# Memory attention and a SiLU feed-forward layer on one core: the gate table by one copy, the first head's loads on another queue, the last sums block by block

## The chip, the core and the metric

The kernel runs on one core of a Trainium2 chip. The core has TensorE (PE in the profile, its weight loads PEld), VectorE (DVE), ScalarE (ACT), GpSimd (POOL) and SyncE (SP). SyncE only issues loads and stores here. SBUF holds the tiles, PSUM the results of TensorE. The metric is the time of one execution in microseconds (us); lower is better.

## The reference

For 8 batches and 8 heads, q, k and v have 576 rows of 64 columns. All is float32.

```python
scores = scale * np.matmul(q, k.transpose(0, 1, 3, 2))        # causal mask, softmax -> a
local = np.matmul(a, v)
q_p = phi(q)                                                   # elu(q) + 1
mem_out = einsum(q_p, M_prev) / (einsum(q_p, z_prev) + 1e-6)
g = 1.0 / (1.0 + np.exp(-beta))                                # one gate for each head
x = g * mem_out + (1 - g) * local                              # -> [4608, 512]
h = x @ w_in                                                   # 512 -> 2048
return (h * (1.0 / (1.0 + np.exp(-h)))) @ w_out                # 2048 -> 512
```

## The kernel before, in words

**Tiles.** A head is worked in `scores` (its softmax and its phi) and `values` (its sums over v and M_prev). Its q and k come in as `raw`, 32 columns at a time, by four loads (L193); DVE transposes the tile (L221, `tt`), and ScalarE copies the q half beside it (L224, `qf`), after which TensorE can start the head's scores (L250). Each block of 128 score rows is reduced on DVE with the mask (L252) and turned into probabilities on ScalarE (L254, the last 64 rows L294). POOL divides them by the sums (L304). `raw` has one buffer, so the four loads of a head wait until the head before has been transposed. There are two PSUM buffers for scores. The first ten heads are worked in plain float32 (`whole`); the others split each operand into a high and a low part.

**The other loads of a head.** `load_rest` issues eight loads for a head: q by rows (`qn`, L201 and L202), v (`vr`, L204 and two at L206), M_prev twice (`mr`, L209) and z_prev (`zb`, L211). All go through SyncE's queue, as the weights do (L138) and all stores. `load_rest` also leaves the last of them in `anchor["sp"]`, behind which the next weight load is placed.

**The gate table.** `bet` holds beta; ScalarE and DVE make 1 + exp(-beta) and 1 + exp(beta) of it (L92 to L95). `over` (L96) repeats these for five blocks of rows and each head: POOL does it in 16 instructions, which add the value to a stretch of `mask` that is zero (L99). `over` is read at L299 and L331.

**Weights.** Each of the 32 weight slices is loaded as 64-bit words, made into float32 by ScalarE (L150, L158), DVE (L152, L154, L159) and POOL (L156), and split in two (L161, L162). Twelve slices go to a scratch in DRAM and flow in again for every block of tokens (`flow`, L485), with two buffers.

**Feed-forward.** 256 tokens are a block; there are 18. For each pair of slices of w_in, TensorE makes h (L552), ScalarE, DVE and POOL make g of it (L563 to L568), and `second` adds g times two slices of w_out to two sums `acc` of 128 tokens each (L532): for each slice c, for each block t of 128 tokens, three products. At the end ScalarE copies both sums (L578) and SyncE stores them (L580).

**What sets the order.** The program is written as generators that take turns: steps of attention, weights at a given rate, and feed-forward at a given rate. A scheduler then orders the instructions of each engine, so any edit can move instructions everywhere. An engine works its instructions in that order. Loads share eight semaphores in turn (DMAHW0 to DMAHW7 in the rows of the order): a load that takes one which an earlier load still holds waits until that load has landed.

## Time and profile before

| | us |
|---|---|
| three runs | 1330.49, 1333.85, 1334.98 (median 1333.85) |
| profiled execution | 1331.87 |
| its span in the profile | 1330.1 |
| TensorE busy | 1269.9 (95%) |
| VectorE busy | 963.4 (72%) |
| ScalarE busy | 805.2 (61%) |
| GpSimd busy | 798.1 (60%) |
| granted TensorE clock, mean | 0.978 |

Times in a profile count from the start of the span. A row of the timeline gives the start, the time taken, the engine with the line, the operation and the tiles (written <- read), how many instructions are merged, and in brackets how long the engine sat idle before it and what it waited for. SPq is SyncE's queue: the row says how long it was issuing, and landing comes later.

### The profile page before, as it was taken

To read this page: it belongs to the slowest core of one execution; us is meant where nothing else is said; L and a number is where in the kernel's file an instruction comes from. 1 tells how busy PE (TensorE), PEld (TensorE's weight loads), DVE (VectorE), ACT (ScalarE), POOL (GpSimd) and SP (SyncE) were. 2 spreads that over 40 slices of the span, in tenths; PEclk is the share of its full clock that TensorE was granted. 3 is DMA by queue.
4 is the path that set the end of the run, shared out by engine and by line. 5 is a ranking of instruction groups with operands and counts; after the bars stand their busy time and mean duration, and the time that the engine had idled before them with its cause. 6 is when DMAs were issued, how large, how long until landed. Compare 5 with 4: busy or idle time off the path is not lost.

```text
span 1330.1 us, 24649 instructions
## 1 busy us (share of the span) xinstructions
PE 1269.9 (95%) x7858; PEld 1084.7 (82%) x7858; DVE 963.4 (72%) x2580; ACT 805.2 (61%) x1999; POOL 798.1 (60%) x1169
## 2 busy tenths in 40 slices
PE   6988989999999999999999999999999999999998
PEld 2343458898989899899989898989898889899997
DVE  7988985788888878877888787778878875322222
ACT  6777765667676767667776676666767663111111
POOL 6888994676666667766677665656576653101110
PEclk9986799999999999999999999999999999999999
DMA  6766555554555545555555455455545432444444
GB/s 163 191 177 176 151 152 159 136 140 134 135 150 137 151 116 135 152 137 151 136 149 140 136 139 136 131 149 136 137 134 145 128 101 80 155 137 155 156 159 143
DMA packets 302994, 190.39 MB, mean 143 GB/s; under 512 B 258832, under 2 KB 267024, under 8 KB 302864
## 3 DMA queue, kind: packets, MB, share of 16 engines
q1 hardware_dynamic: 302864, 188.82, 50.8%
q8 instruction: 62, 1.02, 0.3%
q14 instruction: 68, 0.56, 0.1%
HBM read 173.02 MB, written 15.73 MB: 142 GB/s over the span
## 4 chain that ended last, share of the span: by engine, by line
PE 71%; DVE 13%; ACT 6%; DMA 4%; issue 3%; POOL 2%; SPq 1%; DVEq 0%; POOLq 0%; ACTq 0%
PE h L552 27%; PE acc L532 24%; PE x L422 7%; PE s L250 5%; PE tp L376 4%; DVE s L252 2%; PE x L414 1%; PE tq L351 1%; DMA zb<-in_z_prev 1%; DVE xu L505 1%; DMA flow<-wo_s 1%; DVE th L564 1%; DVE wy L152 1%; DVE wy L159 1%; ACT p L254 1%
## 5 line engine op out<-in xcount | busy, mean ns | idle before, releaser
L552 PE MATMUL h<-xu,wi 128*128 128x256 f32 x2592 | 373.8, 287 | 10.0 <-DVE th L564 7.3
L552 PEld LDWEIGHTS h<-xu,wi 128*128 128x128 f32 x2592 | 342.6, 191 | 24.9 <-DVE th L564 5.9
L304 POOL TENSOR_SCALAR p<-p,st 128x384 f32<-128x384 f32 (+3 forms) x320 | 186.1, 600 | 127.4 <-DVE st L302 121.2
L532 PE MATMUL acc<-wo,g 128*128 128x512 f32 x864 | 244.8, 399 | 0.0
L567 POOL TENSOR_SCALAR g<-th 128x512 fp32r<-128x512 f32 x144 | 90.9, 631 | 236.8 <-DVE th L564 205.7
L532 PE MATMUL acc<-flow,g 128*128 128x512 f32 x864 | 230.9, 395 | 0.7 <-DMA flow<-wo_s 0.7
L254 ACT ACTIVATE p<-s,st 128x128 f32<-128x128 f32 (+3 forms) x256 | 134.9, 528 | 123.2 <-DVE st L252 93.7
L564 DVE SCALAR_TENSOR_TENSOR th<-th,h 128x512 f32<-128x512 f32 x144 | 98.5, 685 | 130.5 <-ACT th L563 128.0
L532 PEld LDWEIGHTS acc<-flow,g 128*128 128x128 f32 x864 | 158.9, 188 | 33.9 <-DMA flow<-wo_s 1.8
L532 PEld LDWEIGHTS acc<-wo,g 128*128 128x128 f32 x864 | 150.0, 189 | 20.1 <-POOL p L304 0.5
L563 ACT ACTIVATE th<-h 128x512 f32<-128x512 f32 x144 | 85.6, 595 | 128.1 <-PE h L552 127.3
L407 DVE TENSOR_TENSOR pl<-tp,ph 128x384 fp32r<-128x384 f32 x216 | 118.4, 550 | 38.1 <-ACT ph L406 33.9
L568 DVE TENSOR_TENSOR g<-th,g 128x512 fp32r<-128x512 f32 x144 | 104.8, 728 | 50.5 <-POOL g L567 49.3
L252 DVE CUSTOM_DVE_ANT_0 s<-s,mask 128x128 f32<-128x128 f32 (+3 forms) x256 | 125.4, 492 | 11.5 <-PE s L250 6.7
L376 PE MATMUL tp<-ident,p 128*128 128x128 f32 x640 | 123.0, 292 | 8.5 <-DVE qp L359 3.7
L552 PE MATMUL h<-xu,flow 128*128 128x256 f32 x864 | 126.7, 284 | 0.0
L406 ACT CAST ph<-tp 128x384 fp32r<-128x384 f32 x216 | 104.7, 490 | 23.6 <-PE x L422 14.7
L552 PEld LDWEIGHTS h<-xu,flow 128*128 128x128 f32 x864 | 114.1, 190 | 0.9 <-issue 0.3
L376 PEld LDWEIGHTS tp<-ident,p 128*128 128x128 f32 x640 | 81.5, 147 | 37.4 <-POOL p L304 9.3
L235 POOL TENSOR_TENSOR ql<-tt,qq 64x512 fp32r<-64x512 f32 x54 | 73.2, 1356 | 20.6 <-ACT qq L231 11.3
L328 POOL TENSOR_TENSOR r<-e,zb 128x320 f32<-128x320 f32 x64 | 59.8, 935 | 42.4 <-DVE e L327 35.4
L422 PE MATMUL x<-pl,vs 128*128 128x256 f32 x324 | 81.7, 307 | 0.0
(103 smaller groups left out, 2430.2 us busy)
## 6 DMA issues: line engine op xcount, KB each, us to landing
flow<-wo_s SPq DMA_DIRECT2D x144, 512.0 KB, 3.5
flow<-wi_s SPq DMA_DIRECT2D x72, 512.0 KB, 3.8
raw<-in_k SPq DMA_DIRECT2D x128, 72.0 KB, 2.3
raw<-in_q SPq DMA_DIRECT2D x128, 72.0 KB, 2.5
out<-o SPq DMA_DIRECT2D x36, 256.0 KB, 4.2
wraw<-in_moe_w_in SPq DMA_DIRECT2D x16, 512.0 KB, 4.4
qn<-in_q SPq DMA_DIRECT2D x64, 128.0 KB, 2.9
vr<-in_v SPq DMA_DIRECT2D x64, 128.0 KB, 2.6
```

The source lines that it names most:

```text
L252: anchor["dve"] = nc.vector.tensor_tensor_reduce(s, s, mask[:, 3 * P - P * i:], QS, 3.0e38, ALU.add, ALU.min, st[:, i:i + 1]).ins
L254: nc.scalar.activation(pt, s, AF.Exp, bias=st[:, i:i + 1], scale=-1.0, accum_out=st[:, 10 + i:11 + i])
L304: nc.gpsimd.tensor_scalar(pb[x], pb[x], st[:, 15 + x:16 + x], 1.0, op0=ALU.mult, op1=ALU.mult)
L376: nc.tensor.transpose(t[:, o:o + P], pb[i][:, P * j:P * j + P], ident)
L406: nc.scalar.copy(ph[:, 0:o], t[:, 0:o])
L407: nc.vector.tensor_tensor(out=pl[:, 0:cut], in0=t[:, 0:cut], in1=f(ph[:, 0:cut]), op=ALU.subtract)
L422: nc.tensor.matmul(x[0:rows, q0:n], vs[0:n_k, j], part[0:n_k, o:o + n - q0], start=False, stop=last)
L532: nc.tensor.matmul(acc[t], ta, tb, start=p == 0 and c == 0 and n == 0, stop=p == NP - 1 and c == 1 and n == len(terms) - 1)
L552: nc.tensor.matmul(h[:, c], ta, tb, start=kk == 0 and n == 0, stop=kk == KD - 1 and n == len(terms) - 1)
L564: nc.vector.scalar_tensor_tensor(out=th, in0=th, scalar=1.0, in1=h, op0=ALU.add, op1=ALU.mult)
L567: nc.gpsimd.tensor_scalar(hi, th, 1.0, 1.0, op0=ALU.mult, op1=ALU.mult)
L568: nc.vector.tensor_tensor(out=lo, in0=th, in1=f(hi), op=ALU.subtract)
```

## The change

Three places change. `over` is now made by one POOL copy from `bet`, broadcast over the five blocks. `load_rest` issues the eight loads of the very first head on ScalarE's queue, and in that case does not set `anchor["sp"]`. In the last pair of slices of the last block of tokens, `second` fetches both slices first and then does all six products of one block of 128 tokens before those of the other; and of the last block's two sums the second is copied by VectorE.

```diff
     over = const.tile([P, 2, H, NQ], F32, name="over")
-    for j in range(2):
-        for hh in range(H):
-            nc.gpsimd.tensor_scalar(over[:, j, hh], mask[:, 0:NQ], bet[:, j, hh:hh + 1], None, op0=ALU.add)
+    nc.gpsimd.tensor_copy(
+        over.rearrange("p j h c -> p (j h) c"),
+        bet.rearrange("p j (h o) -> p (j h) o", o=1).to_broadcast([P, 2 * H, NQ]))
...
     def load_rest(b, h):
+        queue = nc.scalar if b == h == 0 else nc.sync
         qn = qrest[(b * H + h) % 2]
-        nc.sync.dma_start(out=qn[:, 0:NQ - 1], in_=q[b, h, 0:(NQ - 1) * P].rearrange("(c p) d -> p c d", p=P))
+        queue.dma_start(out=qn[:, 0:NQ - 1], in_=q[b, h, 0:(NQ - 1) * P].rearrange("(c p) d -> p c d", p=P))
...
-        anchor["sp"] = nc.sync.dma_start(out=zb, in_=z_prev[b, h:h + 1].to_broadcast([P, D])).ins
+        last = queue.dma_start(out=zb, in_=z_prev[b, h:h + 1].to_broadcast([P, D])).ins
+        if queue is nc.sync:
+            anchor["sp"] = last
...
             def second(p, g):
+                def product(c, t, w):
+                    at = slice(t * P, (t + 1) * P)
+                    terms = [(g[:, gi, c, at], w[:, wi]) for gi, wi in ((0, 0), (0, 1), (1, 0))]
+                    for n, (ta, tb) in enumerate(terms):
+                        nc.tensor.matmul(
+                            acc[t], ta, tb, start=p == 0 and c == 0 and n == 0,
+                            stop=p == NP - 1 and c == 1 and n == len(terms) - 1)
+
+                if u == NU - 1 and p == NP - 1:
+
+                    both = [fetch("o", 2 * p + c) for c in range(2)]
+                    for t in range(T // P):
+                        for c in range(2):
+                            product(c, t, both[c])
+                    return
...
-                nc.scalar.activation(o, acc[t], AF.Copy, scale=0.5)
+                if u == NU - 1 and t % 2:
+                    nc.vector.tensor_scalar(o, acc[t], 0.5, None, op0=ALU.mult)
+                else:
+                    nc.scalar.activation(o, acc[t], AF.Copy, scale=0.5)
```

The scheduler turns this into the following orders. First ScalarE at the program's start, before; the names are the tiles of the sections above, and in brackets stand the semaphores that an instruction waits for.

```order
L93 ACT_TABLE_LOAD [waits DMAHW0_49]
L93 ACTIVATE bet<-bet 128x8 [waits DVE_49]
L94 ACTIVATE bet<-bet 128x8
L224 COPY qf<-tt 64x576 [waits DVE_49]
L150 ACTIVATE wraw<-wraw 128x512 [waits DMAHW5_49]
L325 ACTIVATE e<-qn_146 128x320 [waits DMAHW7_49,DMAHW6_49,Pool_49]
```

And the same place now (line numbers of the changed file are 3 higher from L196 on):

```order
L202 DMA qn_131<-in_q 128x4x64
L203 DMA qn_131<-in_q 64x64
L93 ACT_TABLE_LOAD [waits DMAHW1_49]
L93 ACTIVATE bet<-bet 128x8 [waits DVE_49]
L94 ACTIVATE bet<-bet 128x8
L205 DMA vr<-in_v 128x4x64
L207 DMA vr<-in_v 64x64 x2
L210 DMA mr<-in_M_prev 64x64 [waits DMAHW3_49]
L210 DMA mr<-in_M_prev 64x64 [waits DMAHW5_49]
L212 DMA zb<-in_z_prev 128x64 [waits DMAHW7_49]
L227 COPY qf<-tt 64x576 [waits DVE_49]
L150 ACTIVATE wraw<-wraw 128x512 [waits DMAHW2_49]
```

The eight loads stand ahead of the first head's copy, six of them behind the exponentials of beta, and three of those wait for a semaphore of an earlier load. On SyncE the same eight are gone from between the first and the second weight slice; this is SyncE's start now:

```order
L91 DMA bet<-in_beta 128x8
L193 DMA raw<-in_k 32x18x32 x2
L193 DMA raw<-in_q 32x18x32
L193 DMA raw<-in_q 32x18x32 [waits DMAHW0_49]
L138 DMA wraw<-in_moe_w_in 128x4x128 [waits DMAHW2_49]
L138 DMA wraw<-in_moe_w_in 128x4x128 [waits DMAHW4_49]
L193 DMA raw<-in_k 32x18x32 [waits DMAHW6_49,DMAHW0_49,DVE_49]
L193 DMA raw<-in_k 32x18x32
L193 DMA raw<-in_q 32x18x32 [waits DMAHW1_49]
L193 DMA raw<-in_q 32x18x32 [waits DMAHW2_49]
```

The fourth load of the first head's `raw` now waits for the load that held DMAHW0, which is ScalarE's first; the second head's `raw` waits as before for DVE's transposition, and its last load for the first weight slice.

The second place is ScalarE further on, before: p_218 to p_249 are the first head's probabilities, blocks one to four, and the copy at L224 is the second head's.

```order
L254 ACTIVATE p_218,st<-s,st 128x128
L254 ACTIVATE p_223,st<-s,st 128x256
L161 CAST wi_114<-wy 128x512
L254 ACTIVATE p_233,st<-s,st 128x384
L150 ACTIVATE wraw<-wraw 128x512
L158 ACTIVATE wraw<-wraw 128x512
L254 ACTIVATE p_249,st<-s,st 128x512
L325 ACTIVATE e<-qn_147 128x320
L326 ACTIVATE r<-qn_147 128x320
L356 COPY qp<-tq 64x3x128
L356 COPY qp<-tq 64x2x128
L224 COPY qf<-tt 64x576
```

Now, with p_203 to p_234 for the same four blocks:

```order
L257 ACTIVATE p_203,st<-s,st 128x128
L257 ACTIVATE p_208,st<-s,st 128x256
L161 CAST wi_99<-wy 128x512
L328 ACTIVATE e<-qn_132 128x320
L227 COPY qf<-tt 64x576
L329 ACTIVATE r<-qn_132 128x320
L257 ACTIVATE p_218,st<-s,st 128x384
L158 ACTIVATE wraw<-wraw 128x512
L257 ACTIVATE p_234,st<-s,st 128x512
```

The second head's copy of q has moved from behind the first head's fourth block to ahead of its third.

The third place is TensorE at the program's end, before: wo_142 and wo_144 are slices of w_out that stay in SBUF, flow one that was loaded again.

```order
L532 MATMUL acc<-flow,g 128x512 x6
L532 MATMUL acc<-wo_142,g 128x512 x4
L552 MATMUL h<-xu,flow 128x256 x12
L532 MATMUL acc<-wo_142,g 128x512 x2
L532 MATMUL acc<-flow,g 128x512 x6
L532 MATMUL acc<-wo_144,g 128x512 x6
L532 MATMUL acc<-flow,g 128x512 x6
```

Now:

```order
L533 MATMUL acc<-flow,g 128x512 x6
L565 MATMUL h<-xu,flow 128x256 x12
L533 MATMUL acc<-wo_127,g 128x512 x6
L533 MATMUL acc<-flow,g 128x512 x6
L533 MATMUL acc<-wo_129,g 128x512 x5
L533 MATMUL acc<-flow,g 128x512 x3
L533 MATMUL acc<-wo_129,g 128x512
L533 MATMUL acc<-flow,g 128x512 x3
```

The first block's sum now has its last product four from the end, where it was three from the end.

More of the change, by code (lines that the diff above doesn't have):

```diff
@@ L199, in load_rest @@
     def load_rest(b, h):
+        queue = nc.scalar if b == h == 0 else nc.sync
         qn = qrest[(b * H + h) % 2]
-        nc.sync.dma_start(out=qn[:, 0:NQ - 1], in_=q[b, h, 0:(NQ - 1) * P].rearrange("(c p) d -> p c d", p=P))
-        nc.sync.dma_start(out=qn[0:LAST, NQ - 1], in_=q[b, h, S - LAST:S])
+        queue.dma_start(out=qn[:, 0:NQ - 1], in_=q[b, h, 0:(NQ - 1) * P].rearrange("(c p) d -> p c d", p=P))
+        queue.dma_start(out=qn[0:LAST, NQ - 1], in_=q[b, h, S - LAST:S])
         vr = pool.tile([P, NQ, D], F32, tag="vr", name="vr", bufs=3)
-        nc.sync.dma_start(out=vr[:, 0:NQ - 1], in_=v[b, h, 0:(NQ - 1) * P].rearrange("(c p) d -> p c d", p=P))
+        queue.dma_start(out=vr[:, 0:NQ - 1], in_=v[b, h, 0:(NQ - 1) * P].rearrange("(c p) d -> p c d", p=P))
         for p0 in (0, LAST):
-            nc.sync.dma_start(out=vr[p0:p0 + LAST, NQ - 1], in_=v[b, h, (NQ - 1) * P:S])
+            queue.dma_start(out=vr[p0:p0 + LAST, NQ - 1], in_=v[b, h, (NQ - 1) * P:S])
         mr = pool.tile([P, D], F32, tag="mr", name="mr", bufs=NB["mr"])
         for p0 in (0, 64):
-            nc.sync.dma_start(out=mr[p0:p0 + 64], in_=M_prev[b, h])
+            queue.dma_start(out=mr[p0:p0 + 64], in_=M_prev[b, h])
         zb = pool.tile([P, D], F32, tag="zb", name="zb", bufs=NB["zb"])
-        anchor["sp"] = nc.sync.dma_start(out=zb, in_=z_prev[b, h:h + 1].to_broadcast([P, D])).ins
+        last = queue.dma_start(out=zb, in_=z_prev[b, h:h + 1].to_broadcast([P, D])).ins
+        if queue is nc.sync:
+            anchor["sp"] = last
         return qn, vr, mr, zb
@@ L528, in second @@
                     for t in range(T // P):
-                        at = slice(t * P, (t + 1) * P)
-                        terms = [(g[:, gi, c, at], w[:, wi]) for gi, wi in ((0, 0), (0, 1), (1, 0))]
-                        for n, (ta, tb) in enumerate(terms):
-                            nc.tensor.matmul(
-                                acc[t], ta, tb, start=p == 0 and c == 0 and n == 0,
-                                stop=p == NP - 1 and c == 1 and n == len(terms) - 1)
+                        product(c, t, w)
                     if ("o", 2 * p + c) in FLOW:
```

## The prediction

> **What bounds the kernel now.** I read the page first (busy shares), then the table of windows, then the chain of waits over the first 60 us, then the timeline of the first 24 us and of the last 10 us. The page gives the whole:
>
> ```profile
> PE 1269.9 (95%) x7858; PEld 1084.7 (82%) x7858; DVE 963.4 (72%) x2580; ACT 805.2 (61%) x1999; POOL 798.1 (60%) x1169
> ```
>
> The 95% is an average over stages with different limits. The next rows give, for each stretch, its length, the busy time of each engine with its count of instructions, the granted TensorE clock, the DMA share and GB/s:
>
> ```profile
> 0.00:20.00 20.00, 9.58 (x18) 3.67 (x19) 11.68 (x40) 10.77 (x25) 13.26 (x32) 1.00 0.55 121
> 20.00:60.00 40.00, 36.44 (x81) 14.93 (x81) 36.10 (x85) 28.52 (x68) 32.55 (x29) 1.00 0.73 198
> 80.00:200.00 120.00, 102.58 (x377) 54.29 (x377) 106.53 (x232) 90.39 (x218) 109.72 (x105) 0.79 0.61 168
> 200.00:1100.00 900.00, 876.33 (x5876) 798.71 (x5875) 722.90 (x2059) 616.05 (x1561) 593.60 (x933) 1.00 0.51 138
> 1100.00:1330.00 230.00, 225.35 (x1448) 204.52 (x1447) 70.99 (x129) 43.36 (x92) 33.56 (x57) 1.00 0.43 142
> ```
>
> In the first 20 us no engine is full: PE works 9.58 us, DVE 11.68 us. From 20 to 60 us DVE (36.10 of 40) and PE (36.44) are nearly full; from 80 to 200 us DVE (106.53 of 120) and POOL (109.72) are. From 200 us on PE sets the pace: 876.33 of 900, then 225.35 of 230. So the kernel is a row of full stretches after a start that is not full and before an end of about 4 us without PE. The change touches only the start and the end. What it is worth is how much earlier or later the full stretch begins, and how much sooner the last row is stored.
>
> The chain of waits at the start (start, duration, what):
>
> ```profile
> 10.78 2.38 SPq L193
> ...
> 17.53 0.58 SPq L211
> 18.16 5.21 DMA wraw<-in_moe_w_in
> 23.39 0.43 DVE wy L152
> ...
> 24.39 2.13 POOL p L304 x3
> ```
>
> SP's queue carries the chain: it issues load after load until 18.16 us, then the third w_in slice takes 5.21 us to land, and the normalisation of the first head's probabilities (L304) starts at 24.39 us behind the DVE work on that slice. The timeline of the start has the prices:
>
> ```profile
> 1.45 0.15 POOL L112 MEMSET qn<- 64x64 f32 x1
> 3.79 0.51 SPq L201 DMA_DIRECT2D qn<-in_q  x1
> 4.75 0.19 ACT L94 ACTIVATE bet<-bet 128x8 f32<-128x8 f32 x1
> 4.94 0.58 SPq L204 DMA_DIRECT2D vr<-in_v  x1
> 5.25 5.38 POOL L99 TENSOR_SCALAR over<-mask,bet 128x5 f32<-128x5 f32 x16 [2.35 <-DVE bet L95]
> 5.85 0.78 DVE L221 STREAM_TRANSPOSE tt<-raw 128x576 f32<-128x576 f32 x1 [0.44 <-DMA raw<-in_q]
> 6.66 0.67 ACT L224 COPY qf<-tt 64x576 f32<-64x576 f32 x1 [1.72 <-DVE tt L221]
> 7.38 1.65 PE L250 MATMUL s<-tt,qf 64*128 64x128 f32 x4 [7.38 <-ACT qf L224]
> 8.04 0.58 SPq L211 DMA_DIRECT2D zb<-in_z_prev  x1
> 8.12 0.69 DVE L154 SCALAR_TENSOR_TENSOR wy<-wraw,wy 128x512 uint32<-128x512 uint32 x1
> 9.22 0.97 SPq L193 DMA_DIRECT2D raw<-in_k  x2
> 10.60 1.28 POOL L156 TENSOR_TENSOR wy<-wy,wraw 128x512 uint32<-128x512 uint32 x1
> 13.17 0.58 ACT L254 ACTIVATE p<-s,st 128x384 f32<-128x384 f32 x1
> 15.21 1.07 POOL L334 TENSOR_TENSOR e<-e,nrm 128x320 f32<-128x320 f32 x1 [0.60 <-DVE nrm L333]
> 16.56 0.77 DVE L221 STREAM_TRANSPOSE tt<-raw 128x576 f32<-128x576 f32 x1
> 18.53 0.49 DVE L284 CUSTOM_DVE_ANT_0 pair<-s,mask 64x320 f32<-64x320 f32 x1 [1.20 <-PE s L271]
> 18.66 0.67 ACT L224 COPY qf<-tt 64x576 f32<-64x576 f32 x1
> 23.39 0.43 DVE L152 TENSOR_SCALAR wy<-wraw 128x512 uint32<-128x512 uint32 x1 [0.80 <-DMA wraw<-in_moe_w_in]
> ```
>
> **Gate table.** Sixteen POOL instructions take 5.38 us (L99). One copy of 80 columns replaces them. The trace has no such copy: a 64x64 fill takes 0.15 us and the 128x320 product with a broadcast operand (L334) 1.07 us; I take 0.3 us, a quarter of L334, which has four times the columns. So POOL is freed of about 5.1 us (4.3 to 5.2). What stood behind it is L156, the first weight slice's sum, which began at 10.60 us while its DVE operand was ready at 8.81 us (8.12 + 0.69): at most 1.8 us gained. But L156 also needs ScalarE's L150, and that now stands behind the loads costed next and ends after 10 us. I cost this part at nothing: what covers it is ScalarE. If that cover is gone, it is 1.8 us on one weight slice, of which DVE waits.
>
> **First head's loads on ScalarE's queue.** The order shows two loads ahead of the exp table's load and six between L94 and the first copy of q. ScalarE is done with L94 at 4.94 us (4.75 + 0.19). The same six loads take SP from 4.94 to 8.62 us in the trace (L204 to L211, 8.04 + 0.58), 3.68 us. At SP's price ScalarE reaches its copy at 8.6 us, not 6.66 us. Two of the six also wait for a semaphore that an earlier load holds: the second M_prev load for the first v load. These are landings, from issue, of two v loads of that size (KB each, us to landing), and of the last q quarter of the second head:
>
> ```profile
> vr<-in_v SPq DMA_DIRECT2D x1, 128.0 KB, 3.7
> ...
> vr<-in_v SPq DMA_DIRECT2D x1, 128.0 KB, 2.3
> ...
> raw<-in_q SPq DMA_DIRECT2D x2, 72.0 KB, 4.4
> ```
>
> So v lands at 7.2 to 8.6 us, and the second M_prev load, which would go at 7.4 us, waits up to 1.3 us. The copy starts at 8.6 to 9.9 us: the first score of the kernel comes 2.0 to 3.3 us later, and I take 2.6. If ScalarE issues at almost no cost (no row shows it issuing), the raw loads decide: their last quarter now waits for the first q load's landing (0.72 + 2.3 = 3.0 us) where it was issued at 2.71, so +0.3. The bounds are +0.3 and +3.3. All of the first head is queued behind that copy: PE had nothing before it, and DVE's first reduction waits for PE.
>
> SP in turn is free of eight loads, from 3.79 to 8.62 us, 4.8 us. Not all comes through. The second head's raw tile has one buffer, so its load still waits for the first head's transposition; that ends at 6.63 us (5.85 + 0.78) now and 0.3 to 1 us later after, so the load goes about 2 us earlier than 9.22. Its last quarter then waits for the first w_in slice to land. At 4.4 us to landing the second head's raw is there about 2 us sooner than the trace's 15.2 us (10.78 + 4.4). Behind it SP's eight loads for the second head follow without a gap, and the third w_in slice goes about 4 us before 18.16 us.
>
> The order puts the second head's copy of q ahead of the first head's third exp on ScalarE. That exp now waits for the second head's data: 13.2 us plus 0.78 transposition plus 0.67 copy plus ScalarE's Relu beside it is about 15.5 to 16 us, where the trace has 13.17. So the first head is 2.5 to 3 us late, and the second head's copy, at 15 us for 18.66, is 3 to 4 us early. The two share DVE, which is full from 20 us on. What counts is therefore DVE's idle time until then: +2.6 us before the first reduction; minus the 1.20 us that it waited for PE at 18.53; minus the 0.80 us that it waited for the third w_in slice at 23.39. That is +0.6 us. The bounds: the lane waits at their worst and neither idle saved, +3.3; the whole 4 us by which SP is ahead carried through, -4.
>
> The Trainium skill, "Trainium Kernel Development and Optimization", section "Key Constraints", says that loads issued from SP and ACT run on the same 16 DMA engines, and that issuing from several engines saves only the issue time. The trace agrees so far as it can: a 72 KB load took 4.4 us to land after an issue of half a microsecond. By the rule the gain on SP could be no more than the issue time of the eight loads; it is the reason to doubt the 2 us on the second head's landing, and the second rival prices that.
>
> **End.** The last rows of the timeline and of the chain, an earlier DVE row, and the landing of the last store:
>
> ```profile
> 1301.08 0.69 DVE L564 SCALAR_TENSOR_TENSOR th<-th,h 128x512 f32<-128x512 f32 x1 [6.98 <-ACT th L563]
> ...
> 1325.26 1.29 ACT L578 ACTIVATE o<-acc 128x512 f32<-128x512 f32 x2 [3.99 <-PE acc L532]
> 1325.88 1.03 SPq L580 DMA_DIRECT2D out<-o  x2
> ```
>
> ```profile
> 1321.49 4.44 PE acc L532 x18
> ...
> 1325.95 0.60 ACT o L578
> ```
>
> ```profile
> out<-o SPq DMA_DIRECT2D x1, 256.0 KB, 2.6
> ```
>
> PE does its last 18 products in 4.44 us, 0.247 us each. The second copy starts at 1325.95, right behind PE's last product (1321.49 + 4.44 = 1325.93): ScalarE, done with the first copy by then, did not hold it up. A second engine for it removes a wait that is not there. DVE reading a 128x512 PSUM tile takes 0.69 us (L564), ScalarE 0.60, so that copy is up to 0.1 us longer. By the order, four products instead of three follow the first block's last one, so the first store goes 0.25 us earlier and is less in the way of the second, whose 2.6 us end the run. I take -0.2 us, bounds -0.5 and +0.3. The last weight tile is needed one product sooner; if it is not there, that is 0.25 us more.
>
> **The rest of the program.** The order is shifted everywhere by the scheduler, but heads, weight slices and FFN products keep their places to within a few dozen products. In 200 to 1100 us PE idles 23.7 us of 900; another order of the same work can move this by a few microseconds either way. I take 0, bounds -4 and +4.
>
> **Sum.** +0 (table) + 0.6 (start) - 0.2 (end) + 0 = +0.4 us. The profiled execution took 1331.87 us, its span 1330.1; so 1332.3 by its own time. The median shown, 1333.85, lies 2 us above it; on that, 1334.2 us.
>
> **Rivals.**
> One, SP's lead carries through (faster): third slice and third head arrive 4 us sooner, and so does all that follows the 18.16 us row in the chain. For it: the chain from 10.78 to 23.39 us is SP and a load it issued. Against: DVE's own work in the first 24 us waits on the first head's scores, which come later. Time 1333.85 - 4.0 - 0.2 = 1329.7, on the edge of what can be told; with a favourable order below it.
>
> Two, ScalarE's queue holds the first head up (slower): if the second head's raw lands as late as now, 15.2 us, because the DMA engines and not the issue limit it, its transposition ends at 17.33 us (16.56 + 0.77), its copy at 18.0, and the first head's third exp goes at 18.5 instead of 13.17: +5.3, less the 0.80 saved on the third slice, +4.5 us. Time 1338.4. It decides once that landing is later than about 14.7 us; every microsecond beyond adds one.
>
> Three, the granted clock (slower). This is the wait ahead of the first stretch of the profile with a granted clock below 1:
>
> ```profile
> 86.15 0.79 PE L250 MATMUL s<-tt,qf 64*128 64x128 f32 x2 [3.70 <-DVE st L284]
> ```
>
> PE idled 3.70 us, and from 80 to 200 us the mean granted clock is 0.79, 25 us of full clock lost, most of it beside full DVE and POOL. If the new order puts such an idle at 190 us or later, where PE sets the pace, 10 us at half clock cost 5 us: 1339. For it, every order of those heads is a new draw; against, from 200 us on the clock is 1.00 with PE 97% busy. The Trainium skill, "TensorE: Matmul & The Clock Gate", Part 1, says that an idle window of about 3.4 us halves the clock; the 3.70 us row agrees.
>
> **Chances.** About 0.3%, 4 us, is what a measurement of this kernel can tell from no change. The forecast 0.48, rival one 0.28, two 0.15, three 0.09. Rival one lies at the bound and the forecast's order term reaches over it on both sides; so faster 0.31, within 0.46, slower 0.23. The range takes in rival one with 2.5 us of the order term and two and three: 1327.0 to 1339.5.
>
> **What would show it.** Right: first score near 10 us, second head's copy near 15 us ahead of the first head's third exp, DVE's busy time by 26 us within 1 us of before, the last copy right behind PE's last product, PE idle of 200 to 1100 us near 24 us. Wrong: a first score before 8.5 us (ScalarE issues cheaply), a third w_in slice that no one waits for with L304 of the first head before 22 us (rival one), the second head's raw after 14.7 us (rival two), a granted clock below 1 after 200 us (rival three).

## The result, and the profile after

The changed kernel is slower. Five executions took 1349.08 to 1358.90 us (median 1350.79), the kernel before beside them 1333.61 us (median of six); the ratio of the mean times is 1.0146, 95% interval 1.0116 to 1.0175. The forecast was 1334.2 us, and the range ended at 1339.5. A sixth execution of the changed kernel, at a mean granted clock of 0.469, took 2688.68 us and is in no comparison. The profiled execution took 1358.90 us, the slowest of the five and 8.1 us above their median, so its profile shows more loss than the usual execution has; its span is 1357.1 us, 27.0 longer than before.

The busy shares of the page after:

```profile
PE 1291.7 (95%) x7858; PEld 1094.6 (81%) x7858; DVE 968.3 (71%) x2581; ACT 804.8 (59%) x1998; POOL 794.0 (59%) x1154
```

TensorE runs the same 7858 products, but is busy 21.8 us longer (1291.7 against 1269.9) and idle only 5.3 us longer (65.5 against 60.2). So most of the loss is products that took longer. The same stretches as in the prediction show where (length, busy time of PE, PEld, DVE, ACT, POOL, granted clock, DMA share, GB/s):

```profile
0.00:20.00 20.00, 7.96 (x15) 3.05 (x15) 13.18 (x37) 10.51 (x24) 8.54 (x18) 1.00 0.65 152
20.00:60.00 40.00, 32.55 (x86) 13.65 (x85) 36.13 (x87) 29.23 (x70) 30.82 (x29) 1.00 0.68 181
...
80.00:200.00 120.00, 111.23 (x328) 50.13 (x326) 100.03 (x213) 83.22 (x201) 95.27 (x90) 0.64 0.57 158
200.00:1100.00 900.00, 871.00 (x5775) 790.75 (x5775) 709.55 (x2013) 608.85 (x1538) 598.01 (x930) 0.99 0.51 136
```

From 80 to 200 us the clock fell from 0.79 to 0.64, and 328 products were done where it had been 377. From 200 to 1100 us TensorE did 101 products fewer (5775 for 5876), with 5.3 us more idle time and a clock below 1.

The chain of waits at the start, after (start, duration, what):

```profile
0.73 3.42 DMA qn<-in_q
4.17 0.31 SPq L193
...
4.53 4.54 DMA wraw<-in_moe_w_in
...
13.44 0.77 DVE tt L224
```

SyncE's queue is off it from 9 us on. What heads it is the first load on ScalarE's queue: the fourth `raw` load waits for that one to land (0.73 + 3.42 = 4.15), as the order said it would. The timeline has the rest:

```profile
3.62 0.37 ACTq L205 DMA_DIRECT2D vr<-in_v  x1
...
5.32 0.25 POOL L97 COPY over<-bet 128x80 f32<-128x80 f32 x1 [2.41 <-DVE bet L95]
6.54 0.59 ACTq L212 DMA_DIRECT2D zb<-in_z_prev  x1
...
6.66 0.78 DVE L224 STREAM_TRANSPOSE tt<-raw 128x576 f32<-128x576 f32 x1 [1.40 <-DMA raw<-in_q]
...
7.47 0.67 ACT L227 COPY qf<-tt 64x576 f32<-64x576 f32 x1 [2.42 <-DVE tt L224]
...
8.19 1.64 PE L253 MATMUL s<-tt,qf 64*128 64x128 f32 x4 [8.19 <-ACT qf L227]
...
10.38 1.29 POOL L156 TENSOR_TENSOR wy<-wy,wraw 128x512 uint32<-128x512 uint32 x1 [4.81 <-DVE wy L154]
...
13.44 0.77 DVE L224 STREAM_TRANSPOSE tt<-raw 128x576 f32<-128x576 f32 x1
...
14.56 0.67 ACT L227 COPY qf<-tt 64x576 f32<-64x576 f32 x1
...
15.74 0.43 SPq L138 DMA_DIRECT2D wraw<-in_moe_w_in  x1
...
16.30 0.58 ACT L257 ACTIVATE p<-s,st 128x384 f32<-128x384 f32 x1 [0.58 <-DVE st L255]
...
21.20 0.67 ACT L150 ACTIVATE wraw<-wraw 128x512 uint32<-128x512 uint32 x1 [1.07 <-DMA wraw<-in_moe_w_in]
...
28.19 1.36 POOL L156 TENSOR_TENSOR wy<-wy,wraw 128x512 uint32<-128x512 uint32 x1 [1.56 <-DVE wy L154]
...
30.84 1.69 POOL L156 TENSOR_TENSOR wy<-wy,wraw 128x512 uint32<-128x512 uint32 x1 [1.28 <-ACT wi L161]
...
33.93 3.81 POOL L307 TENSOR_SCALAR p<-p,st 128x128 f32<-128x128 f32 x5
```

The second head's transposition is 3.1 us earlier (13.44 for 16.56), its copy 4.1 us. But the first head's probabilities are divided by their sums at 33.93 us. Before, the same five instructions stand here:

```profile
24.01 3.07 POOL L304 TENSOR_SCALAR p<-p,st 128x128 f32<-128x128 f32 x5 [1.45 <-DVE st L302]
```

That is 9.9 us later, where the head's third exponential is only 3.1 us later (16.30 for 13.17). GpSimd did not wait for these probabilities (the last row of after has no bracket); other work stood ahead of them, and waited itself (L156, 1.56 and 1.28 us). The order of GpSimd, before, behind the first slice's L162:

```
L334 TENSOR_TENSOR e<-e,nrm 128x320
L156 TENSOR_TENSOR wy<-wy,wraw 128x512
L162 TENSOR_TENSOR wi_115<-wy,wi_115 128x512
L328 TENSOR_TENSOR r<-e,zb 128x320
L304 TENSOR_SCALAR p_218<-p_218,st 128x128
```

and after:

```
L337 TENSOR_TENSOR e<-e,nrm 128x320
L156 TENSOR_TENSOR wy<-wy,wraw 128x512
L331 TENSOR_TENSOR r<-e,zb 128x320
L162 TENSOR_TENSOR wi_100<-wy,wi_100 128x512
L337 TENSOR_TENSOR e<-e,nrm 128x320
L156 TENSOR_TENSOR wy<-wy,wraw 128x512 x3
L162 TENSOR_TENSOR wi_101<-wy,wi_101 128x512
L307 TENSOR_SCALAR p_203<-p_203,st 128x128
```

Work on weights and on the second head, whose data now come early, was put ahead of the first head. The end is as forecast:

```profile
1352.52 0.60 ACT L594 ACTIVATE o<-acc 128x512 f32<-128x512 f32 x1 [4.64 <-PE acc L533]
1352.55 0.85 PE L533 MATMUL acc<-flow,g 128*128 128x512 f32 x3
...
1353.44 0.69 DVE L592 TENSOR_SCALAR o<-acc 128x512 f32<-128x512 f32 x1 [3.34 <-PE acc L533]
```

**By heads.** A head begins where DVE transposes its `raw`; I cut both spans at the starts of heads 4, 10, 17, 32, 48 and 63 (counted from 0), so that the pieces hold about the same work. Three of the seven pieces of the table of windows, before:

```profile
0.00:56.77 56.77, 43.00 (x91) 17.35 (x92) 44.62 (x114) 36.13 (x84) 43.23 (x60) 1.00 0.69 180
56.77:156.98 100.21, 86.79 (x269) 40.77 (x269) 86.75 (x207) 78.46 (x190) 85.92 (x77) 0.79 0.63 174
...
511.40:780.81 269.41, 265.42 (x1795) 242.90 (x1794) 220.14 (x634) 189.68 (x480) 186.40 (x290) 1.00 0.53 141
```

and after:

```profile
0.00:52.77 52.77, 34.20 (x74) 13.59 (x75) 42.30 (x107) 33.62 (x78) 35.36 (x43) 1.00 0.68 177
52.77:170.06 117.29, 105.48 (x287) 45.91 (x287) 100.88 (x214) 82.87 (x199) 86.75 (x78) 0.64 0.56 153
...
525.01:803.73 278.72, 268.30 (x1786) 244.63 (x1785) 222.32 (x629) 187.61 (x474) 181.98 (x288) 0.99 0.51 135
```

Head 4 begins 4.0 us sooner, but TensorE has done 74 products by then, not 91. Heads 4 to 10 take 17.1 us longer and hold the missing ones. Heads 32 to 48, a thousand products later and far from anything that was edited, take 9.3 us longer. The pieces differ by -4.0, +17.1, -1.9, +2.4, +9.3, -0.5 and +4.6: +11.2 up to head 17, +15.8 behind it.

### The profile page after: what moved, and what is told of

Same layout as the page of the kernel before. It is cut to its first block, busy times and chain, and to the rows that moved or that the text cites. A ratio compares the mean times of both kernels' runs of the same rounds, so it can differ in the third digit from the quotient of the medians.

```text
span 1357.1 us, 24701 instructions
## 1 busy us (share of the span) xinstructions
PE 1291.7 (95%) x7858; PEld 1094.6 (81%) x7858; DVE 968.3 (71%) x2581; ACT 804.8 (59%) x1998; POOL 794.0 (59%) x1154
## 4 chain that ended last, share of the span: by engine, by line
PE 63%; DVE 16%; POOL 7%; ACT 6%; issue 5%; DMA 2%; SPq 0%; DVEq 0%; POOLq 0%; ACTq 0%
PE h L565 23%; PE acc L533 20%; PE x L425 6%; PE s L253 5%; PE tp L379 4%; POOL p L307 2%; DVE s L255 2%; PE x L417 1%; DVE th L577 1%; DVE pl L410 1%; DVE tt L224 1%; DVE xu L508 1%; PE tq L354 1%; ACT p L257 1%; DVE wy L159 1%
## 5 line engine op out<-in xcount | busy, mean ns | idle before, releaser
L565 PEld LDWEIGHTS h<-xu,wi 128*128 128x128 f32 x2592 | 346.9, 193 | 27.4 <-DVE th L577 7.7
L533 PE MATMUL acc<-wo,g 128*128 128x512 f32 x864 | 240.7, 398 | 0.0
L533 PE MATMUL acc<-flow,g 128*128 128x512 f32 x864 | 234.1, 397 | 0.7 <-DMA flow<-wo_s 0.7
L307 POOL TENSOR_SCALAR p<-p,st 128x384 f32<-128x384 f32 (+3 forms) x320 | 190.1, 613 | 74.3 <-DVE st L305 58.8
L257 ACT ACTIVATE p<-s,st 128x128 f32<-128x128 f32 (+3 forms) x256 | 135.0, 528 | 132.3 <-DVE st L255 118.8
L577 DVE SCALAR_TENSOR_TENSOR th<-th,h 128x512 f32<-128x512 f32 x144 | 98.5, 684 | 118.7 <-ACT th L576 116.7
L576 ACT ACTIVATE th<-h 128x512 f32<-128x512 f32 x144 | 85.7, 595 | 130.1 <-PE h L565 128.9
L581 DVE TENSOR_TENSOR g<-th,g 128x512 fp32r<-128x512 f32 x144 | 109.2, 759 | 51.8 <-POOL g L580 51.0
L379 PE MATMUL tp<-ident,p 128*128 128x128 f32 x640 | 126.0, 292 | 6.0 <-DVE pl L410 1.9
L235 POOL TENSOR_TENSOR kk<-tt,kk 64x576 fp32r<-64x576 f32 x54 | 79.6, 1474 | 6.7 <-ACT kk L233 3.3
L425 PE MATMUL x<-ph,vs 128*128 128x320 f32 (+4 forms) x378 | 80.1, 278 | 3.0 <-POOL vs L319 2.1
```

The lines of the kernel that those rows point to most:

```text
L257: nc.scalar.activation(pt, s, AF.Exp, bias=st[:, i:i + 1], scale=-1.0, accum_out=st[:, 10 + i:11 + i])
L307: nc.gpsimd.tensor_scalar(pb[x], pb[x], st[:, 15 + x:16 + x], 1.0, op0=ALU.mult, op1=ALU.mult)
L379: nc.tensor.transpose(t[:, o:o + P], pb[i][:, P * j:P * j + P], ident)
L425: nc.tensor.matmul(x[0:rows, q0:n], vs[0:n_k, j], part[0:n_k, o:o + n - q0], start=False, stop=last)
L533: nc.tensor.matmul(acc[t], ta, tb, start=p == 0 and c == 0 and n == 0, stop=p == NP - 1 and c == 1 and n == len(terms) - 1)
L565: nc.tensor.matmul(h[:, c], ta, tb, start=kk == 0 and n == 0, stop=kk == KD - 1 and n == len(terms) - 1)
```

## The sum that was tested: idle time and half clock

Durations at half clock are longer, by less than a factor of two in these rows; three transpositions of 128 x 128 in one group, in the timeline after:

```profile
92.69 0.90 PE L379 MATMUL tp<-ident,p 128*128 128x128 f32 x3
...
112.02 0.55 PE L379 MATMUL tp<-ident,p 128*128 128x128 f32 x3
```

So I split every span into TensorE's idle time (span less busy time), half of its busy time at half clock, and the rest. The trace dates each change of the clock. Its windows show 1.00 for the first stretch only because nothing is recorded there: the first record, a return to full clock, comes at 68.0 us before and 50.9 after (the mean clocks of 0.978 and 0.953 leave that time out too), and the time ahead of it is counted as half. The products there bear this out: one transposition of 128 x 128 (L376 of before) takes 421 ns in the median ahead of 68.0 us, 421 ns at a recorded half clock and 272 ns at full clock.

| kernel | span | idle | busy at half clock | span - idle - half of the last |
|---|---|---|---|---|
| before | 1330.1 | 60.2 | 107.9 | 1215.9 |
| after | 1357.1 | 65.5 | 153.8 | 1214.7 |
| queue_alone | 1349.2 | 67.5 | 132.3 | 1215.6 |
| seventeenth_gate | 1352.2 | 64.4 | 144.5 | 1215.5 |
| second_head_on_act | 1347.4 | 74.5 | 122.4 | 1211.6 |
| z_load_on_act | 1342.9 | 56.3 | 147.6 | 1212.9 |
| end_alone | 1333.2 | 59.1 | 118.7 | 1214.7 |
| table_and_tail | 1342.3 | 62.5 | 130.1 | 1214.8 |
| before_128rows | 1341.2 | 86.4 | 78.0 | 1215.8 |
| after_128rows | 1357.6 | 96.8 | 96.0 | 1212.8 |
| rows_fill_on_dve | 1335.1 | 85.9 | 70.8 | 1213.9 |
| rows_and_state_load | 1329.4 | 82.4 | 68.0 | 1213.1 |
| v_loads_on_act | 1338.3 | 60.4 | 125.7 | 1215.1 |
| four_gates_repeated | 1354.0 | 76.7 | 118.1 | 1218.2 |

The rest is 1215 us within 4 in all fourteen kernels. Up to rounding, the 27.0 us between the two profiled executions are 23.0 of half clock (153.8 - 107.9, halved), 5.3 of idle time, and -1.2 of rest. The Trainium skill, "TensorE: Matmul & The Clock Gate", "Terms", prices throttled time by the share of the clock that is withheld. Taken for the busy part of that time alone, the nearly constant last column agrees.

It is an account, not yet a cause: the runs ask what moved it.

## The experiments

The theories: **LOADS**, the moved loads cost the time; **CLOCK**, score products over 64 of the array's 128 rows keep the clock low in the start stage; **ORDER**, any edit at the start makes the scheduler choose another order, and the order sets idle time and clock for the rest. Each kernel was timed in turn with the kernel before, and its ratio is against the executions of before beside it: 7, 17 or 25, which lie at 1329.8 to 1342.0 us (medians 1332.76, 1333.88 and 1334.28). Where the text says that two kernels share an order, the instructions of their traces stand in the same sequence.

**CLOCK, two kernels.** Kernels after and before with the first operand's rows 64 to 127 filled with zeros and read:

```diff
+    qfull = [pool.tile([P, S], F32, tag="kk", name="qf", bufs=QK_BUFS) for _ in range(QK_BUFS)]
+    for t in qfull:
+        nc.gpsimd.memset(t[64:P], 0.0)
...
-            qq = pool.tile([P, S], F32, tag="kk", name="qf", bufs=QK_BUFS)
+            qq = qfull[h % QK_BUFS]
...
-            terms = [(qq[0:64], tt[0:64])]
+            terms = [(qq[0:P], tt[0:P])]
```

> The changed kernel, with the score products of the first ten heads taken over 128 rows instead of 64: the added 64 rows of the q tile are zero, so the sums are the same and PE streams as many columns. Theory clock (the 18 us come from longer stretches at half TensorE clock in the first 190 us, and the clock returns only after a window of 3.4 us in which the array's rows are well used, to which a 64-row product counts half): half-clock stretches end sooner, under 40 us of half clock between 68 and 190 us where the changed kernel has 99, head 17 at least 10 us sooner, time 1328 to 1340. Rival loads (the time is lost to the loads' new places and their waits, the clock is a by-product) and rival busy (the gate counts busy time, whatever the rows): within 4 us of the changed kernel, 1347 to 1356.

> The kernel before, with the same 128-row scores. Theory clock: it has 51 us of half clock between 85 and 175 us and most of the first 68 us; with those cut short, 1318 to 1330, and no longer 18 us but less than 8 away from the changed kernel with 128 rows. Rivals loads and busy: 1330 to 1338, no change that can be told.

Measured: 1357.53 us (ratio 1.0179, 1.0148 to 1.0209) and 1342.82 us (1.0070, 1.0044 to 1.0096). Both lie outside every range that was given, CLOCK's and the rivals'. The clock went the way that the theory says, though less far: full clock first came at 26.5 us for 50.9, and at 28.2 us for 68.0, and busy time at half clock fell by 58 and 30 us, but between 68 and 190 us after_128rows still has 60.9 us at half clock where under 40 was expected. The time did not follow: idle time rose by 31 and 26 us. Heads 4 to 10 in after_128rows:

```profile
55.96:165.00 109.04, 84.75 (x286) 41.67 (x285) 97.36 (x214) 81.28 (x196) 91.41 (x83) 0.75 0.63 172
```

PE is busy 84.75 us instead of 105.48, and the piece is 8.3 us shorter, not 21. In before_128rows the start did gain (start to head 17: 260.0 us for 263.2), but heads 17 to 48 took 533 us for 517.6. Their order was another one, which the edit was not meant to change.

**LOADS against the rest: the parts.** Three kernels take one part of the change each, or leave one out. The first is the kernel before with the change's `load_rest`:

```diff
+        queue = nc.scalar if b == h == 0 else nc.sync
...
-        nc.sync.dma_start(out=qn[:, 0:NQ - 1], in_=q[b, h, 0:(NQ - 1) * P].rearrange("(c p) d -> p c d", p=P))
+        queue.dma_start(out=qn[:, 0:NQ - 1], in_=q[b, h, 0:(NQ - 1) * P].rearrange("(c p) d -> p c d", p=P))
```

> The kernel before with only the first head's loads on ScalarE's queue. Its order differs from before's from the tenth product on, all the way. Theory clock: a new draw of stretches, 1335 to 1355, and the time follows the half-clock time in the first 200 us. Rival loads: the whole loss, 1347 to 1356, also where the clock is as before.

Measured: 1352.15 us, 1.0147 (1.0108 to 1.0187). The loads alone bring the whole loss, but they also bring the change's order: apart from the gate table, the last block and two neighbouring products at 124 us, every engine works in the order of after. So this run does not tell LOADS from ORDER. It does show that the new table and the new end are worth nothing that can be told (1.0147 without them, 1.0146 with them), and it shows one order under another clock. Heads 4 to 10:

```profile
54.15:162.03 107.88, 96.30 (x289) 43.69 (x287) 99.87 (x214) 82.80 (x198) 87.74 (x78) 0.75 0.63 171
```

The piece is 9.4 us shorter than after's 117.29. TensorE's idle time in it is the same (11.6 us for 11.8), its busy time at half clock 62.0 us for 81.3, and half of that difference is 9.6 us. Behind head 17 the two take the same time (1082.8 and 1082.7 us), but queue_alone stands there at 266.4 us, after at 274.4. So 8.0 of the 11.2 us that the profile of after loses ahead of head 17 came without another order; the 15.8 us behind it came with the order.

The second is the change without the loads:

```diff
-        queue = nc.scalar if b == h == 0 else nc.sync
...
-        queue.dma_start(out=qn[:, 0:NQ - 1], in_=q[b, h, 0:(NQ - 1) * P].rearrange("(c p) d -> p c d", p=P))
+        nc.sync.dma_start(out=qn[:, 0:NQ - 1], in_=q[b, h, 0:(NQ - 1) * P].rearrange("(c p) d -> p c d", p=P))
```

> The kernel before with the gate table by one copy and the new end, loads as before. Its order differs from before's only in the first sixth of PE's products. Theory clock: another draw, 1326 to 1345, following the half-clock time of the first 200 us. Rival loads: no loss, 1330 to 1336.

Measured: 1344.76 us, 1.0080 (1.0052 to 1.0108). Without one load moved, 11 us are lost. Its order differs from before's up to product 1942 of 7858, which lies between heads 17 and 32 (the first quarter, not the first sixth). The third is the kernel before with the change's `second` and its copies:

```diff
-                nc.scalar.activation(o, acc[t], AF.Copy, scale=0.5)
+                if u == NU - 1 and t % 2:
+                    nc.vector.tensor_scalar(o, acc[t], 0.5, None, op0=ALU.mult)
+                else:
+                    nc.scalar.activation(o, acc[t], AF.Copy, scale=0.5)
```

> The kernel before with the new end alone; all else stands in before's order. Both theories: 1329 to 1337, no difference that can be told; the second copy starts right behind PE's last product, as before.

Measured: 1334.71 us, 0.9996 (0.9974 to 1.0018). Its order is that of before up to the last products, so its profile shows how far two executions of that order differ: 264.3 us to head 17 for 263.2, 269.3 for heads 32 to 48 for 269.4, and 1068.9 behind head 17 for 1066.9.

**ORDER: an edit of no weight.** The kernel before, with one of its sixteen gate instructions written twice (5.38 / 16 = 0.34 us of GpSimd, the same values again):

```diff
             nc.gpsimd.tensor_scalar(over[:, j, hh], mask[:, 0:NQ], bet[:, j, hh:hh + 1], None, op0=ALU.add)
+    nc.gpsimd.tensor_scalar(over[:, 1, 7], mask[:, 0:NQ], bet[:, 1, 7:8], None, op0=ALU.add)
```

> The kernel before with one instruction repeated: the last of the sixteen gate instructions, 0.34 us on GpSimd, is done twice. Loads, end and table are before's. But its order of products is that of queue_alone in the last 7258 of 7710. Theory order (the time is lost because the scheduler lands in another order, in which PE stalls more often from 500 us on and the clock halves more often): 1343 to 1356, heads 32 to 48 in 277 to 280 us as in the changed kernel, where before takes 269. Rival loads: nothing that can be told from before, 1329 to 1337.

Measured: 1350.65 us, 1.0111 (1.0071 to 1.0152). Heads 32 to 48:

```profile
522.02:799.36 277.34, 266.60 (x1785) 243.17 (x1784) 222.56 (x629) 187.94 (x474) 181.54 (x288) 0.99 0.52 136
```

Both are where ORDER put them. All loads are on SyncE, the table has its sixteen instructions, and behind head 17, where its order is that of queue_alone, the kernel takes 1081.0 us where before takes 1066.9 and after 1082.7.

**ORDER: the change with an order turned back.** Two kernels whose products behind the start stand as in before, or nearly, while loads are moved:

```diff
-        queue = nc.scalar if b == h == 0 else nc.sync
+        queue = nc.scalar if b == 0 and h == 1 else nc.sync
```

> The changed kernel, but ScalarE issues the eight loads of the second head instead of the first; ScalarE's start is the same, with eight loads ahead of its first copy. The order of PE's products is before's in 7208 of 7710, without interruption up to the last block. Theory order: heads 32 to 48 in 268 to 271 us, time 1326 to 1338. Rival loads (issuing on ScalarE costs the time, through its queue or the shared semaphores): 1343 to 1356.

Measured: 1349.38 us, 1.0109 (1.0075 to 1.0142), against 1326 to 1338 expected for ORDER; it lies in the range of LOADS, 1343 to 1356. ORDER missed the total, but the part that the order was to mend was mended. Heads 4 to 10, and heads 32 to 48:

```profile
59.66:175.56 115.90, 98.03 (x285) 42.82 (x283) 95.82 (x214) 82.71 (x198) 88.31 (x83) 0.65 0.58 163
...
530.22:799.56 269.34, 265.37 (x1794) 242.85 (x1793) 220.00 (x632) 189.72 (x480) 186.22 (x290) 1.00 0.53 141
```

Behind head 17 it takes 1066.2 us, as before. All of its loss, 18.0 us, lies ahead of head 17. So there are two losses, and the steady stage's order explains only one. Its first 610 products stand in an order of their own and eight of its loads are moved; no run tells which of the two made the 18.0 us.

Behind head 17 the order decides, and the loads do not. After, queue_alone and seventeenth_gate, which share an order there, take 1082.7, 1082.8 and 1081.0 us with eight, eight and no loads moved. Before, end_alone and second_head_on_act, which share the other, take 1066.9, 1068.9 and 1066.2 with none, none and eight.

The other kernel is the change with seven of its eight loads back on SyncE:

```diff
-        queue.dma_start(out=qn[:, 0:NQ - 1], in_=q[b, h, 0:(NQ - 1) * P].rearrange("(c p) d -> p c d", p=P))
+        nc.sync.dma_start(out=qn[:, 0:NQ - 1], in_=q[b, h, 0:(NQ - 1) * P].rearrange("(c p) d -> p c d", p=P))
...
         last = queue.dma_start(out=zb, in_=z_prev[b, h:h + 1].to_broadcast([P, D])).ins
```

> The changed kernel with only one of the eight loads, z_prev, on ScalarE. PE's order is before's in the last 5877 products (from about head 24 on), another one ahead of that. Theory order: heads 32 to 48 in 268 to 271 us; a draw in the first 24 heads, so 1328 to 1345, as table_and_tail, which shares that order. Rival loads: one eighth of the loss, 1333 to 1337.

Measured: 1342.15 us, 1.0054 (1.0037 to 1.0071), with heads 32 to 48 in 269.3 us. Both within what was expected.

**Both theories together.** The first puts the zeros in by VectorE instead of GpSimd, the second is before_128rows with the first head's M_prev loads on ScalarE:

```diff
-        nc.gpsimd.memset(t[64:P], 0.0)
+        nc.vector.memset(t[64:P], 0.0)
```

> The kernel before with the score products read over 128 rows instead of 64 (rows 64 to 127 of the first operand are filled with zeros once, by VectorE). From about the eight hundredth product on, the products stand in the order that table_and_tail had; the last 5917 stand as in the kernel before. Theory ORDER AND CLOCK: the span is 1211 to 1217 us of products at full clock, plus TensorE's idle time, plus half of its busy time at half clock; the order sets the idle time of the steady stage, the rows in use set when the clock comes back in the start stage. So heads 32 to 48 take 269 to 270 us and heads 17 to 32 take 257 to 259 as in table_and_tail, the first full clock comes before 35 us, half-clock time up to head 17 falls from 125 us to under 105, and the time is 1333 to 1340. Rival (row count is nothing, and whatever made both 128-row kernels slower is the wider product itself): 1345 to 1358.

Measured: 1339.19 us, 1.0032 (1.0011 to 1.0053). In all numbers but one (heads 17 to 32 took 255.2) as expected. Heads 10 to 17, in table_and_tail, then here:

```profile
154.61:265.23 110.62, 106.35 (x580) 81.39 (x579) 77.15 (x201) 72.77 (x182) 77.41 (x100) 0.87 0.53 147
```

```profile
158.37:262.83 104.46, 96.29 (x573) 77.98 (x572) 79.36 (x199) 70.76 (x178) 75.35 (x97) 0.94 0.54 146
```

6.2 us shorter, with 28.6 us at half clock reduced to 12.7 and 3.9 us more idle time. This is not the clock alone: the two share an order only from product 716 on, and heads 10 to 17 are products 364 to 936; in the shared part both take 33.1 us, at full clock. And in heads 4 to 10 the same two kernels take 99.5 and 106.5 us.

```diff
-            nc.sync.dma_start(out=mr[p0:p0 + 64], in_=M_prev[b, h])
+            (nc.scalar if b == h == 0 else nc.sync).dma_start(out=mr[p0:p0 + 64], in_=M_prev[b, h])
```

> before_128rows with one more edit: the first head's two loads of the state matrix are issued by ScalarE. This turns the order of the products back: from about the fifteen hundredth product on they stand as in table_and_tail, the last 5917 as in the kernel before, while without this edit hardly any of them do. Theory ORDER AND CLOCK: heads 32 to 48 go from 274.0 us (before_128rows) to 269 to 270, heads 48 to the end from 548 to 550, and the time from 1342.8 to 1328 to 1340. Rival (moved loads cost time by themselves, and wider products too): 1343 to 1360.

Measured: 1333.96 us, 0.9998 (0.9974 to 1.0023). Moving two loads took 9 us off before_128rows, with heads 32 to 48 at 269.2 us for 274.0. A moved load can thus take time off as well as add it. Behind head 17 it takes 1073.1 us (before: 1066.9), up to it 256.4, the shortest start of all. No kernel was faster than before. The last of the moved loads, v's alone, with the rest of the change:

```diff
         queue.dma_start(out=vr[:, 0:NQ - 1], in_=v[b, h, 0:(NQ - 1) * P].rearrange("(c p) d -> p c d", p=P))
...
-            queue.dma_start(out=mr[p0:p0 + 64], in_=M_prev[b, h])
+            nc.sync.dma_start(out=mr[p0:p0 + 64], in_=M_prev[b, h])
```

> The change, with only the first head's three loads of v on ScalarE's queue; its other loads stay on SyncE's. The products of heads 20 to 55 stand in an order that no run so far had (a third to a half of them in the place that they have in the kernel before), the last ones as in the kernel before up to the change at the end. Theory ORDER AND CLOCK gives no time ahead for an order that has not run: 1333 to 1352, the span of the orders seen; it says that the sum holds, which is that the span less TensorE's idle time less half of its busy time at half clock is 1211 to 1217 us. Rival (the moved loads set the loss, in proportion to how many are moved: three of eight): 1338 to 1343, with heads 32 to 48 at 269 to 272.

Measured: 1340.43 us, 1.0047 (1.0023 to 1.0071), heads 32 to 48 in 269.9 us. It falls where LOADS put it as well as ORDER, so it does not tell them apart. The sum held (1215.1).

The seventeenth gate instruction repeated with three more:

```diff
+    for hh in (4, 5, 6, 7):
+        nc.gpsimd.tensor_scalar(over[:, 1, hh], mask[:, 0:NQ], bet[:, 1, hh:hh + 1], None, op0=ALU.add)
```

> The kernel before with four of the sixteen gate instructions on GpSimd made twice (1.3 us of GpSimd at 5 us of the program), nothing else. Products of heads 17 to 48 stand in the order of queue_alone, those before and behind it in another. Theory ORDER AND CLOCK: heads 32 to 48 take 276 to 280 us instead of 269.4, and the time is 1343 to 1358. Rival (a repeated gate instruction costs what GpSimd spends on it, and seventeenth_gate was a chance of the clock): 1332 to 1338.

Measured: 1358.60 us, 1.0173 (1.0125 to 1.0220), just above the expected 1343 to 1358:

```profile
521.18:800.79 279.61, 269.03 (x1783) 245.35 (x1782) 222.58 (x629) 187.49 (x474) 180.74 (x288) 0.98 0.50 134
```

Its products stand in queue_alone's order from about head 28 to head 49, not from head 17. 1.3 us of GpSimd work at 5 us of the program cost 23 us. No price of an instruction gives that; the order does.

**What a steady-stage order costs.** Waits of TensorE in heads 32 to 48 (total us, times, longest), before:

```profile
PE tp L376 <- DVE pl L407: 1.1, 3, 0.5
...
PE h L552 <- DVE th L564: 0.7, 1, 0.7
```

After, and in seventeenth_gate:

```profile
PE h L565 <- DVE th L577: 5.6, 6, 1.9
PE tp L379 <- DVE qp L362: 1.4, 1, 1.4
```

```profile
PE h L553 <- DVE th L565: 5.6, 6, 1.9
PE tp L377 <- DVE qp L360: 1.4, 1, 1.4
```

Two kernels that have no edit in common wait alike. One of the six waits, after, with DVE's part in it:

```profile
549.42 0.58 ACT L576 ACTIVATE th<-h 128x512 f32<-128x512 f32 x1
...
549.77 0.98 DVE L330 SCALAR_TENSOR_TENSOR e<-e,r 128x320 f32<-128x320 f32 x1
...
550.67 0.55 DVE L255 CUSTOM_DVE_ANT_0 s<-s,mask 128x384 f32<-128x384 f32 x1
...
551.14 0.67 DVE L577 SCALAR_TENSOR_TENSOR th<-th,h 128x512 f32<-128x512 f32 x1
...
551.96 2.33 PE L565 MATMUL h<-xu,wi 128*128 128x256 f32 x12 [1.91 <-DVE th L577]
```

ScalarE's part of `th` is ready at 550.00, but on DVE two instructions for the attention stand ahead, and TensorE sits idle 1.91 us until DVE has freed the PSUM tile of `h`. Then the clock charges it again:

```profile
549.30:552.70 3.40, 1.49 (x12) 1.23 (x11) 3.34 (x8) 2.72 (x8) 3.34 (x6) 1.00 0.87 297
552.70:556.10 3.40, 3.40 (x18) 3.40 (x18) 2.45 (x7) 1.07 (x3) 2.24 (x4) 0.50 0.58 123
```

In 3.4 us PE worked 1.49, and the next 3.4 us ran at half clock. Behind head 17 TensorE is busy at half clock for 23.0 us after and 6.8 before; idle time there rose from 26.0 to 33.6. By the sum that gives 7.6 + 16.2 / 2 = 15.7 us, for 15.8 measured.

## Why the prediction was wrong, point by point

- **Gate table: right.** The copy took 0.25 us, forecast 0.3. L156 went at 10.38 for 10.60, so the 5 us freed on GpSimd were worth nothing there, and queue_alone lost as much without the copy (1.0147) as the change did with it (1.0146). The cover was named wrongly: the row's bracket puts DVE's L154 last, not ScalarE.
- **ScalarE's queue: the wrong path, inside the bounds.** The first score came 0.81 us later (8.19 for 7.38), between the bounds +0.3 and +3.3, not at the 2.6 taken. I let ScalarE issue behind its exponentials; the trace has it issue the first v load at 3.62 us, while the exponentials were still to come, and the last load from 6.54 to 7.13, before the data for its copy were there. Three of the loads wait for a semaphore by the order, not two, but the last six were issued with no more than 0.05 us between them. What held the copy was the path of the lower bound: the fourth `raw` load waited for the first q load, which took 3.42 us to land and not 2.3, and DVE's transposition waited for that `raw`. This was the sign "a first score before 8.5 us".
- **SyncE's lead: right in part.** The second head's copy came at 14.56 (forecast 15), ahead of the third exp at 16.30 (15.5 to 16). But the third slice was issued at 15.74 for 18.16, 2.4 us sooner and not 4, and ScalarE still waited 1.07 us for it. Head 4 began 4.0 us sooner; that this is rival one's price is chance, since TensorE had done 74 products by then and not 91. Rival one's sign, the first head's division before 22 us, failed: 33.93. So did a sign of the forecast: DVE's busy time up to 26 us is 18.91 for 16.37, not within 1 us.
- **The second rival** did not occur: the transposition at 13.44 shows that `raw` had landed before 14.7 us.
- **End: right.** The last copy began right behind PE's last product (1352.55 + 0.85 = 1353.40, copy at 1353.44), and end_alone showed no difference; the 0.2 us of the forecast are too small to be told.
- **The failed step** is the one called "the rest of the program": "another order of the same work can move this by a few microseconds either way. I take 0, bounds -4 and +4." seventeenth_gate and four_gates_repeated, which hold hardly anything but another order, moved the time by 14.8 us (ratio 1.0111) and 23 us (1.0173). In the changed kernel the new order costs 15.8 us behind head 17. The bound had been read from 23.7 us of idle time in 900, as if an order could change only that. It changes the clock as well: of the 15.8 us, 7.6 are idle time and 8.1 are half clock. The rest of the loss lies ahead of head 17, and most of it came with a lower clock under the same order.
- **The third rival** had the mechanism, but at 5 us, from a single idle, and with a limit that did not hold: half clock ahead of 190 us was to lie "beside full DVE and POOL". Up to head 17 the change has 153.3 us at half clock for 119.2 and takes 11.2 us longer. Partly the limit is there: the 128-row kernels show that clock given back in heads 4 to 10 returns in part as waiting. The argument against this rival, a clock of 1.00 from 200 us on, was a rounded mean: before has two stretches of 3.4 us at half clock there, at 463.9 and 870.1 us. Its sign came, a clock of 0.99 from 200 to 1100 us, and the idle time there was 29.0 us, where the forecast's own sign was near 24.

**What stays open.** Ahead of head 17, one order can run at different clocks. In heads 4 to 10, less busy time at half clock made the piece shorter each time, but by different amounts: 9.4 us for 19.3 (queue_alone against after), 4.0 us for 29.4 (table_and_tail against z_load_on_act, whose orders differ in 14 products up to head 10 and in a few instructions of VectorE and ScalarE at the start) and 1.0 us for 8.2 (end_alone against before). In the last two, 7.6 and 2.4 us came back as idle time. Why the clock falls out so differently under one order was not tried. The division of the first head goes with a long start stage but decides nothing alone. With it at 22.7 to 24.3 us head 10 begins at 153.1 to 158.6 us in six kernels (before, end_alone, table_and_tail, z_load_on_act, before_128rows, rows_fill_on_dve), but at 166.9 in seventeenth_gate; with it at 34 to 43 us (queue_alone, after, after_128rows, second_head_on_act) at 162 to 176; and with it at 26.8 to 28.2 us at 152.3 in rows_and_state_load, 163.1 in four_gates_repeated and 164.2 in v_loads_on_act. That this delay is the cause was not tried by itself. Nor is it known by which choice the scheduler comes to the one steady order or the other.

## What to carry to other kernels

Where a scheduler orders the instructions, an edit's price has two parts: its own, which can be read from rows, and a new draw of the order, which cannot. Here the first was under 1 us where a row or a run shows it, and the second up to 23 us, so the range for any edit ahead of a long steady stage has to take it in, and a small gain is only known from the kernel with a neutral edit beside it. When TensorE sets the pace, cost an idle of a microsecond or two also by what it can do to the clock behind it: idle time plus half of the busy time at half clock closed the account within 4 us for fourteen kernels.

## What the runs showed of the hardware

- **A fully busy TensorE can stay at half clock.** From 90 to 105 us after:

```profile
90.00:95.00 5.00, 5.00 (x13) 2.11 (x12) 2.16 (x9) 2.39 (x7) 1.01 (x1) 0.50 0.13 31
95.00:100.00 5.00, 5.00 (x15) 2.42 (x13) 4.85 (x10) 4.05 (x11) 2.53 (x2) 0.50 0.83 234
100.00:105.00 5.00, 5.00 (x10) 1.56 (x9) 4.03 (x11) 2.83 (x7) 4.03 (x5) 0.50 0.72 183
```

  PE is busy 15.00 of 15.00 us and the clock stays at 0.50. The Trainium skill, "TensorE: Matmul & The Clock Gate", Part 1, has the clock return after one busy window of about 3.4 us. The 3.4 us agree (changes of the clock lie 3.41 us or a multiple of it apart); busy time as the measure does not. If each product's busy time is weighted by the rows of the array that it uses out of 128, it fits: of the windows of 3.41 us at half clock in the first 140 us of before and after, the eight that were followed by full clock have 0.88 or more of such busy time, all others 0.87 or less. The score products of the first ten heads use 64 rows. With 128 the clock first came back at 14.0 to 28.2 us in four kernels, with 64 at 43.5 to 68.0 us in ten.
- **A window that is not idle throughout can lose it.** The Trainium skill, "TensorE: Matmul & The Clock Gate", Part 1, asks for an idle window; here stretches with 1.49 us of work in 3.40 (from 549.3 us) and 1.13 in 3.40 (from 692.6) were followed by half clock.
- **ScalarE's loads pass its compute instructions.** The first v load and z_prev took 0.37 and 0.59 us to issue. The v load went at 3.62 us, while the table load ran (3.45 to 4.73) and ahead of two activations, at 4.74 and 4.86, that stand before it in the order. So a load on ScalarE's queue need not keep the place that the order gives it among the compute instructions.
